# Handling keys in pairs in a streamed decode-attention kernel

## The chip, the cores and the metric

The kernel runs on one core of one Trainium2 chip. The metric is device time in microseconds, the median of several executions. The profile is of one execution of the same program; its span, from the first instruction to the last, is about 1.3 us below the device time of that execution. Engines are named as in the profile: PE multiplies matrices (TensorE), DVE is VectorE, ACT is ScalarE, POOL is GpSimd, and SP issues the large loads and the store. In ratios, the mean time of one kernel's fast runs is divided by that of the other's fast runs of the same rounds, so a ratio is not quite the ratio of the medians quoted beside it.

## The reference, cut to what matters

```python
# g = sigmoid(sum(x * gate_w)); out = g * attention(x) + (1 - g) * mixer(x)
q = x @ wq                                  # 32 heads of 128, in 4 groups that share K and V
scores = q k^T / sqrt(128)                  # k_cache: 4 groups x 65536 positions x 128, bf16
a = (softmax(scores) v) @ wo                # v_cache: as large as k_cache
# mixer: gelu(x @ w_in), layernorm of one half, times the other half, @ w_out   (one row)
```

K and V are 67 MB each, and with the weights 162.01 MB have to come from HBM, each byte used once. A "key" in what follows is one piece of 16384 positions of one group, 4.19 MB of K or of V. There are 16 of them, four to a group. A "pair" is two of them, 8.39 MB.

## The kernel before

One queue (SP) issues all large loads, in a fixed order, into a ring of five slots of 4.19 MB. Slots 0 to 2 take K, slots 3 and 4 take V and, at the start, the weights; at the end V12, V13 and wo go into slots 0 to 2 as well. A load is issued when the last reader of its slot is done. The loads go K, V, K, V, a pair at a time:

```python
    for i in range(6):
        a = 2 * i + 4
        if i % 3 == 2:
            load_k(a, 2)
            load_k(a + 1, 0)
        else:
            load_k2(a, (1, 0)[i % 3])
        load_v2(2 * i, VB)
    load_v2(12, SUB)
    ...                                    # v14, v15, then wo in six loads
```

Each key is worked on in four pieces. DVE transposes a piece of K, PE multiplies it with the queries. One key's scores then go from PSUM to SBUF on DVE, with their maximum; exp runs on ACT; DVE transposes the probabilities; PE multiplies them with V ("PV"). All this is spread over the steps of the next keys:

```python
    def k_piece(n, p):
        ...
        P("DVE", lambda e: e.transpose(ktb(i).bitcast(F32), sl[:, 4096 * p:4096 * (p + 1)].bitcast(F32)), ...)
        if p == 3:
            done(("k", n))                 # the slot may be loaded again
        ...                                # PE: 8 matmuls of 512 columns

    def k_step(n, evac=None, gmax=None, pts=(), own=False, mid=None):
        for p in range(4):
            k_piece(n, p)
            if p == 0 and evac is not None:
                score_piece(evac)          # 1024 wide
                ...
            if p == 1 and pts:
                exp_piece(pts[0])
            if p == 2 and pts:
                pt_piece(pts[0]); exp_piece(pts[1])
            if p == 3 and pts:
                pt_piece(pts[1])
            if p == 1 and mid is not None:
                mid()                      # both PV pieces, in the middle of a pair's second key
        ...
```

## Time and profile before

| | before |
|---|---|
| device time, median of 3 | 382.63 us (382.49 to 382.67) |
| span of the profile | 381.5 us |
| bytes read from HBM | 162.01 MB |
| DMA packets' time, share of 16 engines' span | 98.6% |
| PE, DVE, ACT busy | 59%, 55%, 7% |

These are lines of the page of the kernel before: the span, the busy times, the DMA and GB/s rows (40 equal slices of the span; 9 is 90% or more), the queue that loads, and the chain of work that ended last, by engine.

```profile
span 381.5 us, 2501 instructions
...
PE 223.8 (59%) x1375; PEld 54.6 (14%) x785; DVE 210.4 (55%) x229; ACT 25.4 (7%) x39; POOL 1.8 (0%) x9
...
DMA  9999999999999999999999999999989999999995
GB/s 440 433 426 405 440 386 436 437 485 443 428 433 405 405 435 440 440 419 436 443 428 440 440 440 440 435 440 434 440 378 414 460 440 433 433 411 429 417 424 212
...
q1 hardware_dynamic: 4192, 162.01, 98.6%
...
DMA 63%; DVE 21%; PE 13%; SPq 1%; issue 0%; ACTq 0%; DVEq 0%
```

The DMA row is full in every slice but one of 80% and the last. No engine is above 60%. The chain nevertheless gives a third of its length to DVE and PE: at each step it follows what released the next load, and that was a K transpose or a PV matmul that freed a ring slot. This is the timeline of the queue (start, duration, instruction, with the number of DMAs merged into a line) in the middle of the kernel:

```profile
118.88 0.33 SPq L373 DMA_DIRECT2D arena<-in_A_k_cache_dram  x1
134.56 0.33 SPq L373 DMA_DIRECT2D arena<-in_A_v_cache_dram  x1
...
172.99 0.33 SPq L373 DMA_DIRECT2D arena<-in_A_v_cache_dram  x1
...
212.94 0.33 SPq L373 DMA_DIRECT2D arena<-in_A_v_cache_dram  x1
```

Beside these stand the moments at which the completion counts of the loads were full, read from the trace:

```
load      issued   the load ahead of it landed   lead
V0/1       99.38   K4/5    106.93                 7.55
K6/7      118.88   V0/1    126.29                 7.41
V2/3      134.56   K6/7    145.64                11.08
V4/5      172.99   K9      184.42                11.43
V6/7      212.94   K10/11  223.12                10.18
K12/13    234.50   V6/7    242.46                 7.96
V10/11    289.69   K15     301.10                11.41
```

Every load enters the queue 7 us or more before its predecessor has landed. This lead is what an engine may lose without the stream noticing. The costs of what the change touches are in the groups of the profile (operation, shapes, count, busy time and mean ns of one, idle time before them):

```profile
L484 DVE STREAM_TRANSPOSE arena<-arena 128x2048 f32<-128x2048 f32 x64 | 145.0, 2290 | 72.0 <-DMA arena<-in_A_k_cache_dram 62.0
...
L517 ACT ACTIVATE arena<-arena 128x1024 bf16<-128x1024 f32 x16 | 18.4, 1151 | 226.8 <-DVE arena L522 115.7
...
L501 DVE TENSOR_SCALAR_CACHE_REDUCE arena<-scp 128x1024 f32<-128x1024 f32 x16 | 19.1, 1191 | 17.6 <-PE scp L248 17.6
L522 DVE STREAM_TRANSPOSE arena<-arena 128x1024 bf16<-128x1024 bf16 x16 | 19.4, 1214 | 8.9 <-PE obt L248 6.4
```

The four rows are the K transposes, exp, the evacuation of the scores and the transposes of the probabilities.

### The profile page before, as it was taken

The page shows a single profiled execution, that of the slowest core. Times are in us where ns is not written, and L with a number is a line of the kernel's source. Part 1 is how long each engine was busy: PE and PEld are TensorE (multiplying, and loading weights), DVE is VectorE, ACT ScalarE, POOL GpSimd, SP SyncE. Part 2 cuts the span into 40 slices and gives each one's busy share as a digit, 9 for nine tenths or more (in the row PEclk, how much of TensorE's full clock was granted, in tenths as well). Part 3 has the DMA queues.
Part 4 walks back from the last instruction along what each step waited for, and adds up shares of the span by engine and source line. Part 5 has one row for each costly group of instructions (what it writes and reads, how often), then busy time and mean ns, then how long its engine had stood idle before and what let it go on. Part 6 is the DMA issues. An engine that isn't in the chain of part 4 may idle for free.

```text
span 381.5 us, 2501 instructions
## 1 busy us (share of the span) xinstructions
PE 223.8 (59%) x1375; PEld 54.6 (14%) x785; DVE 210.4 (55%) x229; ACT 25.4 (7%) x39; POOL 1.8 (0%) x9
## 2 busy tenths in 40 slices
PE   0060479458456844786756636862779643869373
PEld 0010012011011200121111101210112101212031
DVE  4112596879079606966991069735984990242020
ACT  1000000010212000100210001000300100121000
POOL 1000000000000000000000000000000000000000
PEclk9997599896869995999896969995899995969766
DMA  9999999999999999999999999999989999999995
GB/s 440 433 426 405 440 386 436 437 485 443 428 433 405 405 435 440 440 419 436 443 428 440 440 440 440 435 440 434 440 378 414 460 440 433 433 411 429 417 424 212
DMA packets 4238, 162.16 MB, mean 425 GB/s; under 512 B 508, under 2 KB 516, under 8 KB 772
## 3 DMA queue, kind: packets, MB, share of 16 engines
q1 hardware_dynamic: 4192, 162.01, 98.6%
q8 instruction: 8, 0.13, 0.1%
q14 instruction: 2, 0.02, 0.0%
q10 hardware_dynamic: 36, 0.00, 0.0%
HBM read 162.01 MB, written 0.00 MB: 425 GB/s over the span
## 4 chain that ended last, share of the span: by engine, by line
DMA 63%; DVE 21%; PE 13%; SPq 1%; issue 0%; ACTq 0%; DVEq 0%
DMA arena<-in_A_k_cache_dram 40%; DVE arena L484 16%; DMA arena<-in_A_v_cache_dram 10%; DMA arena<-in_A_wo_dram 8%; DMA arena<-in_B_b_sp_dram 5%; PE obt L246 3%; PE obt L248 3%; PE scp L246 3%; PE scp L248 3%; DVE arena L522 2%; DVE arena L501 1%; SPq L373 0%; ACTq L272 0%; SPq L350 0%; PE scp L427 0%
## 5 line engine op out<-in xcount | busy, mean ns | idle before, releaser
L484 DVE STREAM_TRANSPOSE arena<-arena 128x2048 f32<-128x2048 f32 x64 | 145.0, 2290 | 72.0 <-DMA arena<-in_A_k_cache_dram 62.0
L246 PE MATMUL scp<-arena 128*128 128x512 bf16 x256 | 106.3, 415 | 97.5 <-DVE arena L484 94.2
L248 PE MATMUL scp<-arena 128*128 128x512 bf16 x256 | 104.9, 410 | 0.0
L246 PE MATMUL obt<-arena 128*64 128x512 bf16 (+2 forms) x334 | 63.8, 423 | 22.0 <-DMA arena<-in_A_v_cache_dram 22.0
L248 PE MATMUL obt<-arena 128*64 128x512 bf16 (+2 forms) x334 | 63.1, 418 | 0.0
L246 PEld LDWEIGHTS scp<-arena 128*128 128x128 bf16 x256 | 26.2, 103 | 198.7 <-DVE arena L484 124.6
L517 ACT ACTIVATE arena<-arena 128x1024 bf16<-128x1024 f32 x16 | 18.4, 1151 | 226.8 <-DVE arena L522 115.7
L246 PEld LDWEIGHTS obt<-arena 128*64 128x64 bf16 (+1 forms) x334 | 18.6, 114 | 77.6 <-issue 58.8
L501 DVE TENSOR_SCALAR_CACHE_REDUCE arena<-scp 128x1024 f32<-128x1024 f32 x16 | 19.1, 1191 | 17.6 <-PE scp L248 17.6
L522 DVE STREAM_TRANSPOSE arena<-arena 128x1024 bf16<-128x1024 bf16 x16 | 19.4, 1214 | 8.9 <-PE obt L248 6.4
L547 DVE RECIPROCAL arena<-mbt 128x1 f32<-128x1 f32 x4 | 0.7, 168 | 26.3 <-PE mbt L543 26.3
L731 PE MATMUL fbt<-arena 128*1 128x256 bf16 x128 | 6.4, 364 | 4.0 <-DMA arena<-in_A_wo_dram 3.9
L415 PE MATMUL scp<-arena 8*128 8x1 bf16 x8 | 0.6, 197 | 11.1 <-DVE arena L410 11.1
L420 PE MATMUL mbt<-arena 1*128 1x2 bf16 x1 | 0.2, 158 | 10.1 <-DMA arena<-in_B_b_sp_dram 10.1
L737 DVE CAST arena<-fbt 97x256 bf16<-97x256 f32 x1 | 0.4, 425 | 9.7 <-PE fbt L731 9.7
L422 DVE COPY arena<-mbt 128x2 f32<-128x2 f32 x1 | 0.2, 159 | 10.1 <-PE mbt L420 10.1
L562 PE MATMUL mbt<-arena 128*128 128x128 bf16 x16 | 2.0, 262 | 4.7 <-DVE arena L557 4.7
L731 PEld LDWEIGHTS fbt<-arena 128*1 128x1 bf16 x128 | 3.4, 104 | 7.0 <-DMA arena<-in_A_wo_dram 3.0
L606 ACT ACTIVATE arena<-arena 128x28 f32<-128x28 f32 x1 | 0.2, 228 | 56.7 <-DVE arena L605 56.7
L472 DVE COPY arena<-arena 32x32 bf16<-32x32 bf16 x16 | 2.6, 164 | 2.2 <-PE scp L248 2.0
L449 DVE CAST arena<-obt 97x1024 bf16<-97x1024 f32 x1 | 1.2, 1225 | 4.7 <-PE obt L248 4.7
L568 DVE TENSOR_TENSOR arena<-mbt,arena 128x128 f32<-128x128 f32 x4 | 1.2, 292 | 4.4 <-PE mbt L562 4.4
(89 smaller groups left out, 51.0 us busy)
## 6 DMA issues: line engine op xcount, KB each, us to landing
arena<-in_A_k_cache_dram SPq DMA_DIRECT2D x6, 4096.0 KB, 33.5
arena<-in_A_v_cache_dram SPq DMA_DIRECT2D x2, 4096.0 KB, 23.8
arena<-in_B_w_in_dram SPq DMA_DIRECT2D x1, 7168.0 KB, 30.9
arena<-in_A_wo_dram SPq DMA_DIRECT2D x3, 2048.0 KB, 28.6
arena<-in_B_w_out_dram SPq DMA_DIRECT2D x1, 3584.0 KB, 20.7
arena<-in_A_wo_dram SPq DMA_DIRECT2D x1, 1280.0 KB, 30.9
arena<-in_A_wo_dram SPq DMA_DIRECT2D x1, 512.0 KB, 31.6
arena<-in_A_wo_dram SPq DMA_DIRECT2D x1, 256.0 KB, 31.1
```

What stands on the lines that cost most here:

```text
L246: return e.matmul(*a, **kw)
L248: one = e.matmul(*a, **kw).ins
L449: P("DVE", lambda e: e.tensor_copy(psb[0:97, :], ob[0:97, :]), w=["psb", "ob"])
L472: P("DVE", lambda e, pb=pb: e.tensor_copy(vw(qpad, 24 + 32 * pb, [[QP, 4], [1, 8]], 32 * pb, 32), vw(qall, 8 * g, [[32, 4], [1, 8]], 32 * ...
L484: P("DVE", lambda e: e.transpose(ktb(i).bitcast(F32), sl[:, 4096 * p:4096 * (p + 1)].bitcast(F32)), r=keys[4 * p:4 * p + 4], w=[("kt", i % ...
L501: P("DVE", lambda e: e.tensor_scalar(scs(n), sc_ps(n), 0.0, None, op0=ALU.add, op1=ALU.max, accum_out=maxc[:, n:n + 1]), w=[("sc", n % NSC ...
L517: P("ACT", lambda e: e.activation(psb, scs(n), ACTF.Exp, bias=gcol(n // NP, K_NB), scale=SCALE, accum_out=lp[:, n:n + 1]), r=[("sc", n % N ...
L522: P("DVE", lambda e: e.transpose(ptsb(n), psb), r=["psb"], w=[("ptsb", n % 2)])
L547: P("DVE", lambda e: e.reciprocal(gcol(g, K_RL), mb[:, 0:1]), w=[("rl", g), "mb"])
L562: ins = e.matmul(mb[:, 0:128], sel[:, 128 * c:128 * (c + 1)], osc[:, 128 * c:128 * (c + 1)], start=(c == 0), stop=(c == 3))
L568: P("DVE", lambda e: e.tensor_tensor(vw(ot, 0, [[8, 16], [1, 8]]), vw(mb, 0, [[8, 16], [1, 8]]), vw(mq, 0, [[1, 16], [0, 8]]), ALU.mult), ...
L731: ins = e.matmul(fb[32 * q:32 * q + 1, 0:QW], ovec[:, 8 * i + c:8 * i + c + 1], sl[:, o:o + QW], start=False, stop=(i == 3 and c == 7), ti ...
```

## The change

The intent is fewer and larger operations. Scores of a pair are evacuated in one 2048-wide operation and go through one exp and one transpose. A K pair runs as eight pieces with nothing between them, and the V stage comes behind its K pair instead of in its middle. Ring slots are marked free by key rather than by load. Small operations are merged or move to POOL. The core of the diff, cut:

```diff
-            for x in gr:
-                owner[x] = keys
+            for j, x in enumerate(gr):
+                owner[x] = (keys[j * len(keys) // len(gr)],)
...
-    def score_piece(n):
-        P("DVE", lambda e: e.tensor_scalar(scs(n), sc_ps(n), 0.0, None, op0=ALU.add, op1=ALU.max,
-                                           accum_out=maxc[:, n:n + 1]), w=[("sc", n % NSC), ("mx", n), KSC(n)])
+    def score_pair(j):
+        P("DVE", lambda e: e.tensor_scalar(scs(j), scp[:, :], 0.0, None, op0=ALU.add, op1=ALU.max,
+                                           accum_out=maxc[:, j:j + 1]),
+          w=[("sc", j % 2), ("mx", j), KSC(0), KSC(1)])
...
+    def pt_pair(j):
+        P("DVE", lambda e: e.transpose(ptsb2, psb2), r=["psb"], w=[("ptsb", 0), ("ptsb", 1)])
...
     for i in range(6):
-        a = 2 * i + 4
-        g = i // 2 if i % 2 == 1 else None
-        k_step(a, evac=a - 1, gmax=(a - 1) // NP if a % NP == 0 else None, pts=(2 * i, 2 * i + 1))
...
-        k_step(a + 1, evac=a, mid=mid)
-        if g is not None:
-            out_rest(g)
+        k_step(2 * i + 4)
+        k_step(2 * i + 5)
+        score_pair(i + 2)
+        pv_piece(2 * i)
+        if i % 2:
+            gmax((i + 1) // 2)
+        exp_pair(i + 1)
+        pv_piece(2 * i + 1)
+        if i % 2:
+            out_first(i // 2)
+        pt_pair(i + 1)
+        if i % 2:
+            out_rest(i // 2)
```

More of the change, by code (lines that the diff above doesn't have):

```diff
@@ L166, in bass_gated_mix__gqa_block_cached__mixer_gmlp__decode_kernel @@
     NKT = 2
-    NSC = 5
+    NSC = 4
     QW = DO // 4
@@ L184, in bass_gated_mix__gqa_block_cached__mixer_gmlp__decode_kernel @@
     for name, n in [
-        ("RING", NSUB * SUB), ("KT", NKT * 4096), ("SC", NSC * 2048), ("PSB", 1024), ("PTSB", 2 * 1024),
+        ("RING", NSUB * SUB), ("KT", NKT * 4096), ("SC", NSC * 2048), ("PSB", 2 * 1024), ("PTSB", 2 * 1024),
         ("QPAD", 4 * QP), ("IDB", 128), ("BM", 256), ("SEL", 16 * 32),
         ("M16", 32), ("MQ", 32), ("XT", KC), ("WB", 2), ("WBB", 4), ("ONEB", 128),
-        ("MAXC", 2 * total), ("LP", 2 * total), ("COLS", 2 * 64), ("DM", 32), ("QALL", 128), ("OV", OC), ("MHALF", 4),
+        ("MAXC", 2 * total), ("LP", 2 * total), ("COLS", 2 * 64), ("DM", 64), ("ONES", 256), ("QALL", 128), ("OV", OC), ("MHALF", 4),
         ("YB", FC), ("OROW", QW),
@@ L204, in vw @@
                        ap=[[ps, np_]] + [list(d) for d in dims])
-    idb, bm, ones = ab("IDB", 128), af("BM", 128), af("SC", 128, 4 * 1024 + 896)
+    idb, bm, ones = ab("IDB", 128), af("BM", 128), af("ONES", 128)
     sel, m16, mq = ab("SEL", 512), af("M16", 16), af("MQ", 16)
@@ L212, in bass_gated_mix__gqa_block_cached__mixer_gmlp__decode_kernel @@
     yb, ovec, orow = ab("YB", FC), ab("OV", OC), ab("OROW", QW)
-    dm = af("DM", 16)
-    psb = ab("PSB", 1024)
+    dm = af("DM", 32)
+    psb, psb2 = ab("PSB", 1024), ab("PSB", 2048)
     osc, ot = ab("PSB", 512), af("PSB", 128, 256)
@@ L221, in gcol, with gcol2 @@
         return col(C_G4 + 12 * g + i)
+    def gcol2(g, i):
+        return colt[:, C_G4 + 12 * g + i:C_G4 + 12 * g + i + 2]
     (K_M, K_NB, K_MH, K_L, K_RL, K_F, K_FA, K_FB) = range(8)
     ktb = lambda i: ab("KT", 4096, (i % NKT) * 4096)
-    scs = lambda n: af("SC", 1024, (n % NSC) * 1024)
+    scs = lambda j: af("SC", 2048, (j % 2) * 2048)
     ptsb = lambda i: ab("PTSB", 1024, 1024 * (i % 2))
-    scp = [nc.alloc_psum_tensor("scp%d" % i, [128, 1024], F32) for i in range(2)]
+    ptsb2 = ab("PTSB", 2048)
+    scp = nc.alloc_psum_tensor("scp", [128, 2048], F32)
     obt = nc.alloc_psum_tensor("obt", [128, 1024], F32)
@@ L232, in bass_gated_mix__gqa_block_cached__mixer_gmlp__decode_kernel @@
     fbt = nc.alloc_psum_tensor("fbt", [128, 512], F32)
-    sc_ps = lambda n: scp[n % 2][:, :]
+    sc_ps = lambda n: scp[:, 1024 * (n % 2):1024 * (n % 2 + 1)]
     ob, mb, fb = obt[:, :], mbt[:, :], fbt[:, :]
-    tb = scp[1][:, 0:512]
+    tb = scp[:, 1024:1536]
     tbh = tb.bitcast(BF16)
@@ L249, in mm @@
         return e.add_instruction(dataclasses.replace(one, name=nc.get_next_instruction_name(), ldweights=False))
-    idf = af("SC", 128, 4 * 1024)
-    m8 = af("SC", 8, 4 * 1024 + 128)
-    m32 = af("SC", 32, 4 * 1024 + 136)
-    qT = ab("SC", 32, 4 * 2048 + 400)
+    idf = af("SC", 128, 0)
+    m8 = af("SC", 8, 128)
+    m32 = af("SC", 32, 136)
+    qT = ab("SC", 32, 400)
     P("POOL", lambda e: e.memset(idf, 0.0), w=["idf"])
@@ L261, in bass_gated_mix__gqa_block_cached__mixer_gmlp__decode_kernel @@
     P("POOL", lambda e: e.memset(orow, 0.0), w=["orow"])
-    P("DVE", lambda e: e.memset(ones, 1.0), w=["ones"])
-    P("DVE", lambda e: e.memset(oneb, 1.0), w=["oneb"])
+    P("POOL", lambda e: e.memset(ones, 1.0), w=["ones"])
+    P("POOL", lambda e: e.memset(oneb, 1.0), w=["oneb"])
     P("DVE", lambda e: e.memset(mb, 0.0), w=["mb"])
@@ L272, in f @@
                 return e.dma_start(dst, src)
-        P("ACT", f, w=[key], dma="l%s" % (key if isinstance(key, str) else key[1]))
+        P("ACT", f, w=[key], dma="l" + key)
     xrow, grow, prod = ab("SC", 512, 3 * 2048), ab("SC", 512, 2 * 2048), af("SC", 512, 1 * 1024)
     xm = ab("SC", 1024, 3 * 2048 + 512)
-    KX, KG, KP = ("sc", 3), ("sc", 2), ("sc", 1)
+    KX, KG, KP = "xr", "gr", "pr"
     small(xrow[0:8, 0:128], A_x[0, 0].rearrange("(i n) -> i n", i=8), KX)
@@ L390, in bass_gated_mix__gqa_block_cached__mixer_gmlp__decode_kernel @@
     P("DVE", lambda e: e.tensor_reduce(m16, vw(idf, 0, [[8, 16], [1, 8]]), AXX, ALU.add), r=["idf"], w=["m16"])
-    P("DVE", lambda e: e.tensor_copy(vw(bm, 0, [[8, 16], [1, 8]]), vw(m8, 0, [[0, 16], [1, 8]])), r=["m8"], w=["bm"])
+    P("POOL", lambda e: e.tensor_scalar(m16, m16, -SCALE, None, op0=ALU.mult), r=["m16"], w=["m16"])
+    P("POOL", lambda e: e.tensor_copy(vw(bm, 0, [[8, 16], [1, 8]]), vw(m8, 0, [[0, 16], [1, 8]])), r=["m8"], w=["bm"])
     P("DVE", lambda e: e.tensor_reduce(m32, vw(idf, 0, [[1, 32], [32, 4]]), AXX, ALU.add), r=["idf"], w=["m32"])
-    P("DVE", lambda e: e.tensor_copy(col(C_E4), m32[:, 0:1]), r=["m32"], w=["e4"])
-    P("DVE", lambda e: e.tensor_copy(vw(sel, 0, [[16, 32], [1, 16]]), vw(m32, 0, [[1, 32], [0, 16]])),
+    P("POOL", lambda e: e.tensor_copy(col(C_E4), m32[:, 0:1]), r=["m32"], w=["e4"])
+    P("POOL", lambda e: e.tensor_copy(vw(sel, 0, [[16, 32], [1, 16]]), vw(m32, 0, [[1, 32], [0, 16]])),
       r=["m32"], w=["sel"])
@@ L399, in bass_gated_mix__gqa_block_cached__mixer_gmlp__decode_kernel @@
       r=["idf"], w=["mhalf"])
-    sele = ab("SC", 512, 4 * 2048 + 512)
+    sele = ab("SC", 512, 512)
     KSE = "sele"
     for fe in range(4):
-        P("DVE", lambda e, fe=fe: e.tensor_copy(vw(sele, 128 * fe, [[32, 4], [1, 32]]),
+        P("POOL", lambda e, fe=fe: e.tensor_copy(vw(sele, 128 * fe, [[32, 4], [1, 32]]),
                                                 vw(idb, 64 * (fe // 2) + fe % 2, [[0, 4], [2, 32]])),
@@ L433, in bass_gated_mix__gqa_block_cached__mixer_gmlp__decode_kernel @@
       r=["g"], w=["omg"])
+    P("DVE", lambda e: e.tensor_scalar(mhalf, mhalf, col(C_G), None, op0=ALU.mult), r=["mhalf", "g"], w=["mhalf"])
     wqs, keys = use(("wq", 0))
@@ L471, in q_piece @@
         for pb in range(4):
-            P("DVE", lambda e, pb=pb: e.tensor_copy(vw(qpad, 24 + 32 * pb, [[QP, 4], [1, 8]], 32 * pb, 32),
+            P("POOL", lambda e, pb=pb: e.tensor_copy(vw(qpad, 24 + 32 * pb, [[QP, 4], [1, 8]], 32 * pb, 32),
                                                     vw(qall, 8 * g, [[32, 4], [1, 8]], 32 * pb, 32)),
@@ L504, in max_first @@
     def max_first(g):
-        P("DVE", lambda e: e.tensor_reduce(gcol(g, K_M), maxc[:, NP * g:NP * (g + 1)], AXX, ALU.max),
-          r=[("mx", NP * g + u) for u in range(NP)], w=[("m", g)])
-        P("DVE", lambda e: e.tensor_scalar(dm, m16, gcol(g, K_M), None, op0=ALU.mult), r=["m16", ("m", g)], w=["dm"])
-        P("PE", lambda e: e.matmul(mb[:, 0:16], bm, dm, start=True, stop=True), r=["bm", "dm"], w=["mb"])
+        P("DVE", lambda e: e.tensor_tensor(vw(dm, 0, [[16, 2], [1, 16]]), vw(m16, 0, [[0, 2], [1, 16]]),
+                                           vw(maxc, 2 * g, [[1, 2], [0, 16]]), ALU.mult),
+          r=["m16", ("mx", 2 * g), ("mx", 2 * g + 1)], w=["dm"])
@@ L511, in max_second @@
+        P("PE", lambda e: e.matmul(mb[:, 0:32], bm, dm, start=True, stop=True), r=["bm", "dm"], w=["mb"])
     def max_second(g):
-        P("DVE", lambda e: e.tensor_reduce(gcol(g, K_MH), mb[:, 0:16], AXX, ALU.max), w=[("mh", g), "mb"])
-        P("DVE", lambda e: e.tensor_scalar(gcol(g, K_NB), gcol(g, K_MH), -SCALE, None, op0=ALU.mult),
-          r=[("mh", g)], w=[("nb", g)])
-    def exp_piece(n):
-        P("ACT", lambda e: e.activation(psb, scs(n), ACTF.Exp, bias=gcol(n // NP, K_NB), scale=SCALE,
-                                        accum_out=lp[:, n:n + 1]),
-          r=[("sc", n % NSC), ("nb", n // NP)], w=["psb", ("lp", n)])
@@ L521, in pt_piece, with exp_pair @@
-    def pt_piece(n):
-        P("DVE", lambda e: e.transpose(ptsb(n), psb), r=["psb"], w=[("ptsb", n % 2)])
+        P("DVE", lambda e: e.tensor_reduce(gcol(g, K_NB), mb[:, 0:32], AXX, ALU.min), w=[("nb", g), "mb"])
+    def exp_pair(j):
+        P("ACT", lambda e: e.activation(psb2, scs(j), ACTF.Exp, bias=gcol(j // 2, K_NB), scale=SCALE,
+                                        accum_out=lp[:, j:j + 1]),
+          r=[("sc", j % 2), ("nb", j // 2)], w=["psb", ("lp", j)])
+    def pt_pair(j):
+        P("DVE", lambda e: e.transpose(ptsb2, psb2), r=["psb"], w=[("ptsb", 0), ("ptsb", 1)])
@@ L524, in pv_piece, with pt_half @@
+    def pt_half(n):
+        P("DVE", lambda e: e.transpose(ptsb(n), ab("PSB", 1024, 1024 * (n % 2))), r=["psb"], w=[("ptsb", n % 2)])
     def pv_piece(n):
@@ L540, in out_first, with f @@
     def out_first(g):
-        P("DVE", lambda e: e.tensor_reduce(gcol(g, K_L), lp[:, NP * g:NP * (g + 1)], AXX, ALU.add),
-          r=[("lp", NP * g + u) for u in range(NP)], w=[("l", g)])
-        P("PE", lambda e: e.matmul(mb[:, 0:1], bm, gcol(g, K_L), start=True, stop=True),
-          r=["bm", ("l", g)], w=["mb"])
+        def f(e):
+            for h in range(2):
+                ins = e.matmul(mb[:, 0:1], bm, lp[:, 2 * g + h:2 * g + h + 1], start=(h == 0), stop=(h == 1))
+            return ins
+        P("PE", f, r=["bm", ("lp", 2 * g), ("lp", 2 * g + 1)], w=["mb"])
     def out_second(g):
         P("DVE", lambda e: e.reciprocal(gcol(g, K_RL), mb[:, 0:1]), w=[("rl", g), "mb"])
-        P("DVE", lambda e: e.tensor_scalar(gcol(g, K_F), gcol(g, K_RL), col(C_G), None, op0=ALU.mult),
-          r=[("rl", g), "g"], w=[("f", g)])
-        for h, k in ((0, K_FA), (1, K_FB)):
-            P("DVE", lambda e, h=h, k=k: e.tensor_scalar(gcol(g, k), mhalf[:, h:h + 1], gcol(g, K_F), None, op0=ALU.mult),
-              r=[("f", g), "mhalf"], w=[("fh", g, h)])
+        P("DVE", lambda e: e.tensor_scalar(gcol2(g, K_FA), mhalf, gcol(g, K_RL), None, op0=ALU.mult),
+          r=[("rl", g), "mhalf"], w=[("fh", g)])
     def out_third(g):
         P("DVE", lambda e: e.tensor_scalar(osc, ob[:, 0:512], gcol(g, K_FA), None, op0=ALU.mult),
-          r=[("fh", g, 0)], w=["psb", "ob"])
+          r=[("fh", g)], w=["psb", "ob"])
         P("DVE", lambda e: e.scalar_tensor_tensor(osc, ob[:, 512:1024], gcol(g, K_FB), osc, op0=ALU.mult, op1=ALU.add),
-          r=[("fh", g, 1), "psb"], w=["psb", "ob"])
+          r=[("fh", g), "psb"], w=["psb", "ob"])
         def f(e):
@@ L591, in mixer_piece @@
         NZ = 2 * FB4
-        zr, zt = af("SC", NZ, 3 * 1024), af("SC", NZ, 4 * 1024)
-        KZR, KZT = ("sc", 3), ("sc", 4)
-        zw = lambda i: af("SC", 28, 3 * 1024 + 32 * i)
+        zr, zt = af("SC", NZ, 2 * 1024), af("SC", NZ, 3 * 1024)
+        KZR, KZT = ("sc", 1), "zt"
+        zw = lambda i: af("SC", 28, 2 * 1024 + 32 * i)
         zc = vw(zt, 0, [[32, 28]])
@@ L644, in wout_piece @@
         done(("wout", 0))
-        part = scs(4)
-        P("ACT", lambda e: e.activation(part[0:97, :], ob[0:97, :], ACTF.Copy), w=[("sc", 4), "ob"])
+        part = ab("KT", 2048, 4096).bitcast(F32)
+        P("ACT", lambda e: e.activation(part[0:97, :], ob[0:97, :], ACTF.Copy), w=[("kt", 1), "ob"])
         def f(e):
@@ L652, in f, with k_step, gmax @@
             return ins
-        P("PE", f, r=["e4", ("sc", 4)], w=["fb"])
-    def k_step(n, evac=None, gmax=None, pts=(), own=False, mid=None):
+        P("PE", f, r=["e4", ("kt", 1)], w=["fb"])
+    def k_step(n):
         for p in range(4):
             k_piece(n, p)
-            if p == 0 and evac is not None:
-                score_piece(evac)
-                if gmax is not None:
-                    max_first(gmax)
-            if p == 1 and gmax is not None:
-                max_second(gmax)
-            if p == 1 and pts:
-                exp_piece(pts[0])
-            if p == 2 and pts:
-                pt_piece(pts[0])
-                exp_piece(pts[1])
-            if p == 3 and pts:
-                pt_piece(pts[1])
-            if p == 1 and mid is not None:
-                mid()
-        if own:
-            score_piece(n)
+    def gmax(g):
+        max_first(g)
+        max_second(g)
     def out_rest(g):
@@ L683, in bass_gated_mix__gqa_block_cached__mixer_gmlp__decode_kernel @@
     k_step(0)
-    k_step(1, evac=0, own=True)
+    k_step(1)
+    score_pair(0)
     mix = mixer_piece()
@@ L687, in bass_gated_mix__gqa_block_cached__mixer_gmlp__decode_kernel @@
     mixer_rest(*mix)
-    k_step(3, evac=2)
+    k_step(3)
+    score_pair(1)
     wout_piece()
+    gmax(0)
+    exp_pair(0)
+    pt_pair(0)
     for i in range(6):
-        a = 2 * i + 4
-        g = i // 2 if i % 2 == 1 else None
-        k_step(a, evac=a - 1, gmax=(a - 1) // NP if a % NP == 0 else None, pts=(2 * i, 2 * i + 1))
-        if i == 5:
-            k_step(a + 1, evac=a, own=True, mid=lambda: pv_piece(10))
-            max_first(3)
-            max_second(3)
-            exp_piece(12)
-            pv_piece(11)
-            out_first(2)
-            pt_piece(12)
-            out_rest(2)
-            continue
-        def mid(i=i, g=g):
-            pv_piece(2 * i)
-            pv_piece(2 * i + 1)
-            if g is not None:
-                out_first(g)
-        k_step(a + 1, evac=a, mid=mid)
-        if g is not None:
-            out_rest(g)
-    exp_piece(13)
-    pt_piece(13)
+        k_step(2 * i + 4)
[11 more added lines that the diff above has]
+            out_rest(i // 2)
+    exp_pair(7)
     for n in (12, 13, 14, 15):
@@ L717, in bass_gated_mix__gqa_block_cached__mixer_gmlp__decode_kernel @@
         if n < 14:
-            exp_piece(n + 2)
-            pt_piece(n + 2)
+            pt_half(n + 2)
     out_first(3)
```

## The prediction

> **What bounds the kernel now.** The page gives 382.6 us (span 381.5) and 162.01 MB read from HBM; the DMA queue's packets fill 98.6% of the span of 16 engines. Spread over the packets' own times, the 4 us windows from 4 to 372 us all show 16 transfers in flight and 426 to 434 GB/s: the stream is never short of work. The Trainium skill, "DMA: Bandwidth & Descriptors", Specifications, puts the fabric ceiling at 435 GB/s; this trace touches 434. At 434 the bytes alone need 373.3 us. The rest is about 2 us before the stream is up, some 2 us of slightly slower windows and the tail: last wo landing 378.9, matmuls, cast, store, end at 381.5. Engines have room: DVE 210 us (55%), PE 224 (59%), ACT 25. The chain of waits names K transposes (16%) and PE, but only because it follows the release of a ring slot; the queue then has earlier transfers in hand.
>
> **How much in hand.** By the queue's own instructions and the landings, each load is issued 7 to 13 us before the one ahead of it lands (V0/1 issued 99.4, K4/5 lands 106.9; K6/7 118.9, V0/1 126.3; V4/5 173.0, K9 184.4; V10/11 289.7, K15 301.1). An engine change matters only if it eats that lead.
>
> **What the change does, costed.** Sixteen 1024-wide evacuations (1.19 + 0.08 us) become eight of about 2.3; sixteen exps (1.15 + 0.19) become eight of about 2.2; sixteen bf16 transposes (1.21) become seven of 2.3 and two single ones; some small operations go; the 0.16 us query copies and some setup move to POOL. DVE should lose 5 to 9 us of 210. None of it is on the limiting resource. The bytes, their order and the last 2 us stay. Freeing slots by key changes when the program may record a load; the dependency (the last reader of the slot) was already the one key: K6/7 goes at 118.88, when K4's last transpose ends, not K5's.
>
> **The lead afterwards.** A pair lands at t. Eight transposes at 2.2 us plus about 3 us of half-clock PE (3.4 instead of 1.9 us a piece at first): last K matmul about t+21.5. V landed at t+19.4. Both PV pieces take 7.1 us together at full clock (127.4 to 134.5), so V is free about t+29 (now t+27.3: 145.6 to 173.0); the deadline is t+38.7. The pair transpose ends about t+31, out_rest (5 us) by t+36, before the next pair lands. K's first key is free at about t+11, as now (11.9). So leads stay 7 to 12 us and the stream does not run dry. The tail still waits for wo: the last group's output is ready at 369.7, wo lands until 378.9.
>
> **Prediction.** 382.5 us, range 381.6 to 383.5. Faster by over 2%: 0.01; within 2%: 0.97; slower by over 2%: 0.02.
>
> **What would show it.** DMA packets again about 98.6% of the span, every slice but first and last full; the queue's issues 7 us or more ahead of the previous landing; V issues 1 to 3 us later; last wo landing within 0.5 us of 378.9; DVE busy about 203 us; ACT about 22.
>
> **What would make it wrong.** DVE waiting in the pair transpose for PV, then starting the next K pair so late that a V load is issued after the queue has drained: slices below 9 in the DMA row would show it, 3 us each. Or POOL's copies stalling PE at group starts. A gain over 2 us would need a shorter head or tail; I see no cause.

## The result

The changed kernel takes 382.39 us (382.27 to 382.53, 6 runs); the kernel before took 382.6 us (382.49 to 382.75, 6 runs) in the same rounds. The ratio is 0.9994, with a 95% interval of 0.9982 to 1.0007: the same. The page of the changed kernel, the same lines:

```profile
span 381.1 us, 2468 instructions
...
PE 229.2 (60%) x1383; PEld 55.5 (15%) x793; DVE 204.5 (54%) x162; ACT 22.2 (6%) x23; POOL 7.5 (2%) x35
...
DMA  9999999999999999999999999999999999999995
GB/s 440 434 433 413 426 387 437 440 492 420 428 433 392 426 442 440 433 420 433 454 428 440 440 440 440 421 433 440 392 420 439 457 433 426 426 408 433 423 430 223
...
q1 hardware_dynamic: 4192, 162.01, 98.7%
...
DMA 63%; DVE 18%; PE 17%; issue 1%; ACTq 0%; SPq 0%; DVEq 0%
```

DVE has lost 5.9 us and ACT 3.2 us. The DMA row is full in every slice but the last, the share is 98.7%. In the chain, 3 to 4% of the span went from DVE to PE; the way of the chain between two loads changed, the loads did not. These are its groups, the same four operations and the two single transposes at the end:

```profile
L490 DVE STREAM_TRANSPOSE arena<-arena 128x2048 f32<-128x2048 f32 x64 | 142.8, 2283 | 45.9 <-DMA arena<-in_A_k_cache_dram 31.3
...
L527 DVE STREAM_TRANSPOSE arena<-arena 128x2048 bf16<-128x2048 bf16 x7 | 16.2, 2311 | 31.3 <-PE obt L252 29.1
...
L522 ACT ACTIVATE arena<-arena 128x2048 bf16<-128x2048 f32 x8 | 16.0, 2003 | 218.1 <-DVE arena L519 195.0
L507 DVE TENSOR_SCALAR_CACHE_REDUCE arena<-scp 128x2048 f32<-128x2048 f32 x8 | 18.3, 2292 | 16.0 <-PE scp L252 16.0
...
L530 DVE STREAM_TRANSPOSE arena<-arena 128x1024 bf16<-128x1024 bf16 x2 | 2.5, 1245 | 12.7 <-PE obt L252 12.7
```

The pair sizes cost nearly twice the single ones: 2292 ns for 1191, 2311 for 1214. About 0.1 us is saved each time. Only exp gains more, 2003 ns against two of 1151. On DVE the merged evacuations and transposes, with the short reads of the maxima, save 2.1 us in all; the sixteen query copies that moved to POOL were 2.6 us, which is more. The Trainium skill, "ScalarE: Activation LUTs", What ACT_TABLE_LOAD costs, gives about 280 ns and 0.833 ns an element for an operation with a bias operand. That makes an estimate of 1133 and 1986 ns, and this trace agrees within 2%. DVE's idle time in front of the pair transposes is mostly new: 31.3 us in total, where the single ones had 8.9. The waits of DVE (total, times, longest) before and after show what it is exchanged for:

```profile
DVE arena L484 <- DMA arena<-in_A_k_cache_dram: 62.0, 6, 21.8
```

```profile
DVE arena L490 <- DMA arena<-in_A_k_cache_dram: 31.3, 6, 10.2
DVE arena L527 <- PE obt L252: 29.1, 6, 9.1
```

DVE waited 62.0 us for K to land; now it waits 31.3 us for K and 29.1 us for PV, 60.4 us together. About half of the time in which DVE waited for the stream is now a wait for PE. The queue's timeline in the changed kernel, the same four issues as before:

```profile
117.89 0.33 SPq L377 DMA_DIRECT2D arena<-in_A_k_cache_dram  x1
135.67 0.33 SPq L377 DMA_DIRECT2D arena<-in_A_v_cache_dram  x1
...
174.34 0.33 SPq L377 DMA_DIRECT2D arena<-in_A_v_cache_dram  x1
...
212.40 0.33 SPq L377 DMA_DIRECT2D arena<-in_A_v_cache_dram  x1
```

With the landings of this trace, K6/7 has a lead of 8.14 us, V2/3 9.87, V4/5 9.98, V6/7 10.62. The shortest in the whole kernel is 6.96 us (K4/5). The last piece of wo lands at 378.45 us; before it was 378.91.

### The profile page after: what moved, and what is told of

It is laid out like the page before. It is cut to its first block, busy times and chain, and to the rows that moved or that the text cites. A ratio compares the mean times of both kernels' runs of the same rounds, so it can differ in the third digit from the quotient of the medians.

```text
span 381.1 us, 2468 instructions
## 1 busy us (share of the span) xinstructions
PE 229.2 (60%) x1383; PEld 55.5 (15%) x793; DVE 204.5 (54%) x162; ACT 22.2 (6%) x23; POOL 7.5 (2%) x35
## 3 DMA queue, kind: packets, MB, share of 16 engines
q1 hardware_dynamic: 4192, 162.01, 98.7%
## 4 chain that ended last, share of the span: by engine, by line
DMA 63%; DVE 18%; PE 17%; issue 1%; ACTq 0%; SPq 0%; DVEq 0%
DMA arena<-in_A_k_cache_dram 41%; DVE arena L490 15%; DMA arena<-in_A_v_cache_dram 10%; DMA arena<-in_A_wo_dram 8%; PE scp L250 5%; DMA arena<-in_B_b_sp_dram 5%; PE scp L252 5%; PE obt L250 3%; PE obt L252 3%; DVE arena L527 1%; PE fbt L718 1%; ACTq L276 0%; DVE arena L563 0%; DVE arena L561 0%; SPq L377 0%
## 5 line engine op out<-in xcount | busy, mean ns | idle before, releaser
L490 DVE STREAM_TRANSPOSE arena<-arena 128x2048 f32<-128x2048 f32 x64 | 142.8, 2283 | 45.9 <-DMA arena<-in_A_k_cache_dram 31.3
L250 PE MATMUL scp<-arena 128*128 128x512 bf16 x256 | 108.9, 425 | 84.9 <-DVE arena L490 84.9
L252 PE MATMUL scp<-arena 128*128 128x512 bf16 x256 | 107.7, 421 | 0.0
L250 PE MATMUL obt<-arena 128*64 128x512 bf16 (+2 forms) x334 | 62.8, 416 | 21.3 <-DMA arena<-in_A_v_cache_dram 21.3
L252 PE MATMUL obt<-arena 128*64 128x512 bf16 (+2 forms) x334 | 61.9, 410 | 0.0
L527 DVE STREAM_TRANSPOSE arena<-arena 128x2048 bf16<-128x2048 bf16 x7 | 16.2, 2311 | 31.3 <-PE obt L252 29.1
L522 ACT ACTIVATE arena<-arena 128x2048 bf16<-128x2048 f32 x8 | 16.0, 2003 | 218.1 <-DVE arena L519 195.0
L507 DVE TENSOR_SCALAR_CACHE_REDUCE arena<-scp 128x2048 f32<-128x2048 f32 x8 | 18.3, 2292 | 16.0 <-PE scp L252 16.0
L530 DVE STREAM_TRANSPOSE arena<-arena 128x1024 bf16<-128x1024 bf16 x2 | 2.5, 1245 | 12.7 <-PE obt L252 12.7
L478 POOL COPY arena<-arena 32x32 bf16<-32x32 bf16 x16 | 3.3, 204 | 236.3 <-PE scp L252 210.9
L519 DVE TENSOR_REDUCE arena<-mbt 128x1 f32<-128x32 f32 x4 | 0.8, 192 | 13.3 <-PE mbt L516 13.3
L415 DVE TENSOR_TENSOR arena<-arena 8x1024 bf16<-8x1024 bf16 x1 | 1.2, 1211 | 4.9 <-DMA arena<-in_A_x_dram 4.9
## 6 DMA issues: line engine op xcount, KB each, us to landing
arena<-in_A_wo_dram SPq DMA_DIRECT2D x1, 256.0 KB, 31.3
```

The lines of the kernel that those rows point to most:

```text
L250: return e.matmul(*a, **kw)
L252: one = e.matmul(*a, **kw).ins
L415: P("DVE", lambda e: e.tensor_tensor(vw(xm, 0, [[128, 8], [1, 128]], 0, 8), vw(xrow, 0, [[0, 8], [1, 128]], 0, 8), vw(idb, 0, [[1, 8], [0, ...
L478: P("POOL", lambda e, pb=pb: e.tensor_copy(vw(qpad, 24 + 32 * pb, [[QP, 4], [1, 8]], 32 * pb, 32), vw(qall, 8 * g, [[32, 4], [1, 8]], 32 * ...
L507: P("DVE", lambda e: e.tensor_scalar(scs(j), scp[:, :], 0.0, None, op0=ALU.add, op1=ALU.max, accum_out=maxc[:, j:j + 1]), w=[("sc", j % 2) ...
L519: P("DVE", lambda e: e.tensor_reduce(gcol(g, K_NB), mb[:, 0:32], AXX, ALU.min), w=[("nb", g), "mb"])
```

## The experiments

Theory A says that the stream of loads sets the time and that the engines only have to keep a lead. Rival B says that the engines' chain sets a good part of it, as the chain of work suggests, and that the change's saving was cancelled by a new wait. Ten kernels were run, each timed in three rounds against the kernel before, which took 382.4 to 382.6 us each time.

Even without the attention work the result passed, so the attention part of the output must be small against what the comparison tolerates. Correctness therefore tells little in this section.

### The loads alone

All K, V and softmax operations are left out; the slots are simply freed in the old order.

```diff
-    k_step(0)
-    k_step(1)
-    score_pair(0)
+    P("POOL", lambda e: e.memset(ovec, 0.0), w=[("ovec", g) for g in range(4)])
+    done(("k", 0))
+    done(("k", 1))
     mix = mixer_piece()
...
-        k_step(2 * i + 4)
-        k_step(2 * i + 5)
-        ...                                 # and all the rest of the pass
+        done(("k", 2 * i + 4))
+        done(("k", 2 * i + 5))
+        done(("v", 2 * i))
+        done(("v", 2 * i + 1))
```

> The changed kernel with every K, V and softmax operation left out (the loads, the gate, the mixer, the wo stage and the store stay; the result is wrong on purpose). Theory A, the stream of loads sets the time: the floor of the same bytes is 380.5 to 382.5 us, within 0.5% of the changed kernel. Rival B, the engines' chain (K transposes and PE name a third of the chain that ended last) sets a good part of the time: 320 to 370 us.

Measured: 382.09 us (ratio to before 0.9986, 0.9971 to 1.0). The page's busy times, DMA row, queue and chain:

```profile
PE 27.2 (7%) x319; PEld 8.9 (2%) x241; DVE 13.5 (4%) x41; ACT 4.2 (1%) x6; POOL 4.3 (1%) x20
...
DMA  9999989999999999999999999999999999999995
...
q1 hardware_dynamic: 4192, 162.01, 98.7%
...
DMA 94%; PE 5%; ACTq 0%; DVE 0%; issue 0%; SPq 0%; DVEq 0%
```

With DVE at 4% and PE at 7% the kernel is 0.3 us shorter than the changed kernel. All attention work of either kernel costs about 0.5 us beyond the stream, 1.1 us at the far end of the interval. This settles A for the whole, and it bounds what any further engine schedule could gain.

### Slots freed by whole loads again

```diff
-            for j, x in enumerate(gr):
-                owner[x] = (keys[j * len(keys) // len(gr)],)
+            for x in gr:
+                owner[x] = keys
```

> The changed kernel, with ring slots freed by the whole load again as before. My theory: the queue's order and the last reader of a slot are the same, so every load is issued within 0.5 us of where the changed kernel issues it, and the time is 382.4 within 0.3. Rival: freeing by key lets a load go one key (about 11 us) earlier; undone, leads of 7 to 10 us turn negative and the time grows by 2 to 20 us.

Measured: 382.22 us (ratio 0.9989, 0.9974 to 1.0004). K6/7 was issued at 117.29 us against 117.89 in the changed kernel, K12/13 at 233.45 against 234.06, K14 at 252.06 against 252.66. Most issues are within 0.6 us; V6/7 came 1.7 us earlier, and the loads of w_in, K2, V14, V15 and wo came 0.8 to 1.0 us earlier or later. The 0.5 us expected was too narrow, for these and for the 0.6 us above. None moved by the 11 us of a key. The mark in the program decides only where a load is recorded. The wait that the chip sees is on the last reader of the slot, which was the one key in both versions.

### More work on DVE, in two doses

```diff
         pt_pair(i + 1)
+        for _ in range(2):                  # 5 in the second kernel
+            P("DVE", lambda e: e.transpose(ptsb2, psb2), r=["psb", ("ptsb", 0)], w=[("ptsb", 0), ("ptsb", 1)])
```

> The changed kernel with the pair transpose repeated twice more in each of the six loop passes: six times 4.7, 28 us more DVE work on the path that holds up the next pair. Theory A, by a recurrence of the measured stage times: the lead of the loads absorbs it, 382.4 within 1 us, shortest lead of a V load 5 to 9 us. Rival B: up to 28 us more, about 410.

> The same, with five repeats: six times 11.75, 70 us more DVE work. Theory A: the pair's loop (33.5 us on average and 11.75) is longer than the 38.7 us in which two loads arrive, so the lead is used up after the second pair and the queue runs dry; the recurrence gives 26 us more, about 408 (400 to 416), with slices below 9 in the DMA row. Rival B: 70 us more, about 452.

Measured: 382.60 us with two repeats (ratio 0.9998, 0.9981 to 1.0014) and 403.72 us with five (ratio 1.0547, 1.0532 to 1.0563). The first dose, 28 us of work, costs nothing that the interval shows; the shortest lead of a V load issued after the first repeat is 9.1 us, and that of K10/11 fell from 13.3 to 8.3. The second dose, 70 us, costs 21 us, where the recurrence had said 26 and rival B 70. The page of the larger dose:

```profile
PE 219.5 (55%) x1383; PEld 53.3 (13%) x793; DVE 273.5 (68%) x192; ACT 22.2 (6%) x23; POOL 7.5 (2%) x35
...
DMA  9999999999999999899959996999996995999995
...
q1 hardware_dynamic: 4192, 162.01, 94.3%
...
DVE 46%; DMA 27%; PE 25%; issue 1%; SPq 1%; ACTq 0%; DVEq 0%
```

Four slices of the DMA row fall to 5 or 6, one for each load that was late, and DVE takes 46% of the chain. This is how a stream looks that really waits for the engines. The late loads: K10/11 was issued 2.0 us after its predecessor had landed, K12/13 1.3, V10/11 1.9, V12/13 3.2. Each of them landed 4.3 to 6.1 us later than a queued load would have, so a late load costs its lateness and a further 2.4 to 3.6 us. Its first packets start 1.0 us after the issue; how the rest comes about is not shown. In the same trace, V6/7 with a lead of 4.2 us landed 19.53 us after its predecessor, nearly as the loads with long leads do (19.36). A shorter lead may not be enough: in the traces of the engine schedules below, loads of wo that were issued 0.9 to 3.5 us before their predecessor landed came 0.6 to 2.2 us later after it than in the changed kernel. There the stream had just begun again, so the lead alone is not shown to be the cause.

### Fewer bytes

V14 and V15 are not loaded; V12 and V13 are used again.

```diff
-    load([("v", 14)], kv(A_v_cache, 14), VB)
-    load([("v", 15)], kv(A_v_cache, 15), VB + SUB)
+    place[("v", 14)], place[("v", 15)] = place[("v", 12)], place[("v", 13)]
...                                          # and slots of v12, v13 are freed when v14, v15 are done
```

> The changed kernel without the loads of V14 and V15 (V12 and V13 are used again, so the arithmetic has the same size and the result is wrong on purpose): 8.39 MB of 162.01 less, all engine work kept. Theory A: 8.39 MB at 434 GB/s, 19.3 us less, 363.1 within 1. Rival B, engines on the path: less than 10 us less.

Measured: 370.03 us (ratio 0.9675), 12.4 us below the changed kernel, not 19.3. This was a miss, and the edit was at fault. The reused V12/13 held ring slot 1, in which wo2 and wo3 were to go, so wo2 was issued at 351.78 us, 2.69 us after wo1 had landed, and landed at 359.43. The kernel was run again with wo2 and wo3 in the slot that V10 leaves:

```diff
-    WO_AT = [0, 8 * DO, 16 * DO, 24 * DO]
+    WO_AT = [0, 8 * DO, VB, VB + 8 * DO]
```

> less_bytes, mended: there wo2 and wo3 lay in the ring slot that the reused V12/13 held until PV of V14, so wo2 was issued 2.7 us after the load before it had landed and the stream ran dry for about 5 us. Here they go to the slot that V10 leaves. Theory A: the stream is whole again, last wo landing 19.3 us earlier than in the changed kernel (378.45), at 359.2 within 0.5; the time is 19.3 us below 382.4, 363.1, plus up to 1.6 us because the last PV pieces (end 355.2) and the wo matmuls now end at about the same time: 363 to 365. Rival B: the landing moves by less than 15 us.

Measured: 365.71 us (ratio 0.9552; the profile is of the slowest of five executions, 367.24 us). The last landing moved from 378.45 to 359.03, by 19.42 us. The time followed by only 16.7 and is 0.7 us above the expected range, because the end of the work is now on the path: the last PV matmul ends at 355.8, the last group's output is ready at 359.8, and the wo matmuls end at 363.7. Taking 5% of the bytes away was enough to uncover the engines at the tail.

### The engine schedules without the stream

K0/1 and V0/1 are loaded once and used for all keys, in the kernel before, in the changed one, and in the changed one with PV put back into the middle of the second key. The weights are still loaded at the start and at the end.

```diff
-    load_k(2, 2)
-    load_k(3, 0)
...
-    load([("v", 15)], kv(A_v_cache, 15), VB + SUB)
+    load_v2(0, VB)
+    for n in range(2, 16):
+        place[("k", n)], place[("v", n)] = place[("k", n % 2)], place[("v", n % 2)]
```

The third has in addition:

```diff
-        k_step(2 * i + 5)
-        score_pair(i + 2)
-        pv_piece(2 * i)
+        for p in range(4):
+            k_piece(2 * i + 5, p)
+            if p == 1:
+                pv_piece(2 * i)
+                pv_piece(2 * i + 1)
+        score_pair(i + 2)
         if i % 2:
             gmax((i + 1) // 2)
         exp_pair(i + 1)
-        pv_piece(2 * i + 1)
```

> The kernel before with K0/1 and V0/1 loaded once and used for all sixteen keys (wrong on purpose): the engine schedule without the stream. Stages of the traces: a pair takes 29.5 us (even) and 32.7 (odd) from its first transpose to the next pair's; six of them after about 100 us of start, 25 us of end: about 315 us (305 to 330). That the time is far below 382 is Theory A; Rival B says over 365.

> The same for the changed kernel. If its saved DVE time made its engine schedule faster, it would be 5 to 10 us below engines_before. My theory: a pair takes 31.4 (even) and 34.2 us (odd), because DVE's pair transpose waits for PV and PV for the whole pair, so it is about 10 us slower than engines_before, about 325 (312 to 340), and the stream hides that.

> engines_after with both PV pieces put back into the middle of the second key (after its second piece, as in the kernel before), the rest paired. Two K pieces then wait behind PV on PE, and the one evacuation, the maximum, exp and pair transpose follow them: 2 to 3 us a pair slower than engines_after, about 340. If the V stage's new place alone were what costs, it would be 5 to 10 us faster than engines_after.

Measured: 317.54 us (314.51 to 318.16), 325.77 us (324.83 to 326.53) and 342.51 us (341.71 to 345.4). The busy times and the DMA row of the first two:

```profile
PE 212.5 (67%) x1375; PEld 52.4 (17%) x785; DVE 210.4 (66%) x229; ACT 25.3 (8%) x39; POOL 1.8 (1%) x9
...
DMA  9999999137004993000000000000000009891000
```

```profile
PE 220.6 (68%) x1383; PEld 53.7 (17%) x793; DVE 203.9 (63%) x162; ACT 22.2 (7%) x23; POOL 7.5 (2%) x35
...
DMA  9998999082009850000000000000000006991000
```

The changed kernel has 6.5 us less DVE work and takes 8.2 us longer. Its PE is busy for 8.1 us more with eight more matmuls, at a mean granted clock of 0.884 against 0.925; how much of the 8.2 us lies in that clock was not separated. The intervals between the first K transposes of successive pairs, from the traces, show where:

```
from pair    K0-2    K2-4    K4-6    K6-8    K8-10   K10-12  K12-14
before      28.50   29.91   32.02   32.23   29.44   32.23   29.68
after       26.38   36.98   30.66   34.20   30.68   34.18   30.68
after, mid  27.31   37.28   32.76   38.43   31.79   38.90   32.00
```

The expectation had the total about right and its parts only roughly. Five passes of the loop cost 4.8 us together, 7.1 us come from the step before the loop, where the evacuation, exp and the transposes of the first pair now run before K4 may begin, and 4.4 us are won back at the start and at the end. The comparison flatters the changed kernel in one place: in the kernel before PE waits 2.5 us for V0/1 to land in the first pass (32.02 us, where passes of its kind take 29.4 to 29.7), in the changed one not at all. Without this wait the loop would cost about 7 us, by an estimate from these intervals.

The last row of the table is from the slowest of its four executions (345.4 us). By the medians the middle place costs 17 us more than the place behind the K pair, and the paired kernel with PV in the middle, which differs in small operations too, takes 25 us more than the kernel before. The groups of the transposes of the probabilities and of the evacuations show why, first in the changed kernel's schedule, then with PV in the middle:

```profile
L521 DVE STREAM_TRANSPOSE arena<-arena 128x2048 bf16<-128x2048 bf16 x7 | 16.2, 2311 | 27.0 <-PE obt L252 24.8
...
L501 DVE TENSOR_SCALAR_CACHE_REDUCE arena<-scp 128x2048 f32<-128x2048 f32 x8 | 18.3, 2292 | 16.0 <-PE scp L252 16.0
```

```profile
L501 DVE TENSOR_SCALAR_CACHE_REDUCE arena<-scp 128x2048 f32<-128x2048 f32 x8 | 18.3, 2292 | 53.3 <-PE scp L252 53.3
...
L521 DVE STREAM_TRANSPOSE arena<-arena 128x2048 bf16<-128x2048 bf16 x7 | 16.2, 2309 | 8.7 <-ACT arena L516 8.7
```

With PV behind the K pair, the pair transpose waits for PV. With PV in the middle that wait is gone, but the one evacuation waits for the K pieces that PE does after PV, 53.3 us instead of 16.0. So the change's parts are not independent: once the scores are handled in pairs, the new place of PV is the better one.

### PV in the middle, with the stream

The same edit in the changed kernel with all its loads.

> The changed kernel with both PV pieces back in the middle of the second key, the part of the change that puts the V stage behind its K pair undone alone. Its engine schedule is 17 us slower by itself (engines_after_mid 342.5 against engines_after 325.8), with pairs of 32 and 38.5 us against 38.7 us of loads. Theory A: hidden, 382.4 within 0.6, every lead still over 4 us. Rival B: 5 to 17 us slower.

Measured: 382.34 us (ratio 1.0, 0.9985 to 1.0015). The shortest lead among the loads of the loop falls to 4.92 us (K10/11), the last landing is at 378.38. Engine schedules of 317.5, 325.8 and 342.5 us all give 382.3 to 382.6 us under the stream.

No experiment points to an engine schedule that would beat both kernels by more than about half a microsecond: the loads alone take 382.1 us. What was not tried is to shorten the two ends of the stream.

## Why the prediction was right

The prediction was 382.5 us, 381.6 to 383.5; the time is 382.39.

- *The stream is never short of work, so engine time is free.* Shown: without the attention work the time is 382.09, with 28 us more of it 382.60, and with 8.39 MB less the last landing comes 19.42 us earlier.
- *The leads stay 7 to 12 us.* The shortest is 6.96, and outside the single K loads, which are issued early, the longest of the loop is 13.3. The hand-made sequence for a pair that lands at t held closely. For K6/7, landing at 145.54, the last K matmul ended at t+21.3 (predicted 21.5), V was free at t+28.8 (29), the pair transpose ended at t+31.2 (31), and the output stage at t+34.3 (36).
- *V issues come 1 to 3 us later.* In part: V2/3, V4/5 and V8/9 came 1.1, 1.4 and 2.1 us later, V0/1 and V10/11 0.2 and 0.4 later, and V6/7 0.5 earlier.
- *Freeing by key changes only the record.* Shown by undoing it alone.
- *DVE about 203, ACT about 22.* They are 204.5 and 22.2.
- *The half-clock start of a pair.* The prediction took 3 us for it. The Trainium skill, "TensorE: Matmul & The Clock Gate", What's actually happening, describes an idle PE at half clock that speeds up after about 3.4 us of work. In two pairs of the kernel before, the records show the granted clock going from 0.5 to 1.0 at 3.0 and at 5.2 us after the pair's first matmul (109.33 to 112.31, 148.03 to 153.27): around the page's figure, but not one fixed time.
- *What it named as risks.* In the changed kernel no V load was issued after the queue had drained, and the waits of the changed kernel's trace show none of PE for POOL.
- *What the prediction left out.* It did not say what the engine schedule is worth by itself. Without the stream the saving of DVE time would not have made the kernel faster either: as a schedule the changed kernel is 8.2 us slower than the one before. The stream hides the loss as it would have hidden a gain.

The 0.2 us between the medians is inside the interval and is not explained here.

## What to carry to other kernels

When loads form one stream, measure how long before the landing of its predecessor each load enters the queue. Here this lead said what a slower or faster engine could change, and the chain of work that ended last did not. Two kernels settle it cheaply: one with the loads alone, which gives the floor, and one with the loads taken away, which gives the engines' own time. Busy time saved by merging operations may cost overlap, because a merged operation waits for the last of its inputs; here the pair transpose and the pair evacuation did.

## What the Trainium skill lacked or had wrong

- "DMA: Bandwidth & Descriptors", Where 436 GB/s comes from, says without a condition that for HBM to SBUF the HBM side (about 358 GB/s) binds. In the kernel before, the one core in use reads from HBM at 426 to 434 GB/s in every 4 us window from 4 to 372 us, close to the 435 of the fabric. The same page elsewhere, and the page "HBM Reference", Specifications (TRN2), have it right for a core that streams alone (about 425).
- Beyond a fixed cost of a single DMA, no page says how early a load has to be queued so that a stream has no gap, nor what a late one costs. Here a lead of 4.2 us left hardly any (0.2 us), and loads issued 1.3 to 3.2 us late cost that and 2.4 to 3.6 us more.
- No page warns that the chain of work that ended last can name engines which only released a buffer early: it gave 34 to 35% of the span to DVE and PE in two kernels whose medians are 0.5 and 0.3 us above that of the loads alone.
